# One attention group's transposes through DRAM, eight weight sums four steps earlier, and four weight sums ahead of a copy

## The chip, the cores and the metric

The kernel runs on one core of one Trainium2 chip. The metric is device time in microseconds (us), the median of three runs. Times on the trace's axis are microseconds from the start of the profiled span.

## The reference

Chunked attention (4 batches, 8 heads, 576 positions, head width 64, chunks of 64) feeds two MLPs in turn, on 2304 tokens of width 512.

```python
scores = scale * np.matmul(q_c, k_c.transpose(0, 1, 2, 4, 3))
attn = np.exp(scores - scores.max(-1))            # then divided by its row sum
x = np.matmul(attn, v_c)                          # as (2304, 512)
h = x @ w_in                                      # 512 x 2048
x = (np.maximum(h, 0) + alpha * np.minimum(h, 0)) @ w_out
out = ((x @ w_a) * (x @ w_b)) @ w_o               # 512 x 1536, 1536 x 512
```

The weights come as 64-bit floats. Every product is made of three matmuls on a high and a low part of its operands.

## The kernel before

**Order.** The kernel writes its order by hand: each engine does its instructions in the order in which the code issues them. All DMAs are issued by SP, in that order too. The 2304 tokens are five blocks (512, 256, 512, 512, 512 tokens; numbers 0 to 4). In the first stage, blocks 0, 1 and 2 pass through the first MLP in 16 steps j each: `s1(j)` is the product with `w_in`'s part j (into a PSUM bank `psh`), `prelu` makes `gh` and `gl` of it (ACT `neg` and `pos`, DVE `pos`, ACT `gh`, DVE `gl`), and `s2(j)`, two steps later, multiplies them by `w_out`'s part j into `acc`. Then blocks 3 and 4 pass as a pair through `group1(jp)`, eight groups that need seven products where eight would be plain. They work on sums and differences of the weights (`t_steps`) and of the inputs (`y_sums`). The second MLP and its own groups follow.

**Attention in block 2.** While block 2 runs, `att_line` does the attention of the last eight groups of 128 tokens (units 10 to 17, `us[0]` to `us[7]`). Its tables give a slot to each piece of work; step j calls the slots 2j and 2j + 1. For a unit, `load_kq` loads k and q into a staging buffer, `apart` (ACT `kqd`, two activations) parts each number into its two 16-bit halves and writes them to DRAM (`rowsk`, `rowsq`), `turn_qk` reads them back as DMA transposes (`kT`, `qT`), `multiply` does the scores on PE (`psSO<-kT,qT`; called S below, S15 for unit 15), `soften` the softmax. The sixth, unit 15 (`us[5]`), is the exception: `att_kq` (line 310) transposes its k and q on PE at slot 13, into two of the four `ps` banks, and ACT copies them out.

**Weight sums.** `w_in`'s parts in one piece, high plus low, are needed again by `group1`. `keep_sum(j)` adds them on DVE (line 161, tile `wi`), `keep_out(n)` writes the next n sums to DRAM (`wd`). Parts 0 to 7 are summed in block 1. In block 2, lines 1336 to 1340 sum part j at the end of step j for j = 8 to 15, and write one sum at step 0 and up to two at each of the steps 11 to 15. `load_raw(jp)` reads two of them back (`wir`).

**First pair group.** `group1(0)` (from line 1428) is where the pair begins: `soon` holds the high and low part of one weight tile for the next group (`Txh`, `Txl`), `more` the four sums (`wit`) and the remaining parts (`txh`, `txl`). `p5` and `t2` share a staging buffer; there are three such buffers, and `end1(2)` has just used two of them for block 2's result (`xs`, written out as `x2d`).

**Buffers.** 72 tiles of 128x512 hold weights, attention and sums alike; a new tile waits until the last reader of its buffer is through.

Of the kernel before, what the change touches and what calls it, by code (L numbers as in the profile page):

```python
# [18 lines left out]
def chunk_attention_prelu_mlp_bilinear_mlp(  # L19
# [27 lines left out]
    J1 = F1 // P  # L47
# [38 lines left out]
    def to_hi(hi, lo, src):  # L86
        nc.scalar.activation(out=hi, in_=src, func=AF.Copy)  # L87
# [69 lines left out]
    def keep_sum(j):  # L157

        hi, lo = W["i", j]
        x = wtile("wi", F32)  # L160
        nc.vector.tensor_tensor(out=x, in0=hi.bitcast(F32), in1=lo.bitcast(F32), op=ALU.add)
        whole.append((j, x))

    def keep_out(n):
        for _ in range(min(n, len(whole))):
            j, x = whole.pop(0)
            nc.sync.dma_start(out=wd[j], in_=x)
# [48 lines left out]
    att = {}  # L216
# [83 lines left out]
    def att_T(u, nms="kq"):  # L300
        for nm in nms:
            src = att.pop((nm, u))
            ps = att_bank(u, "psT")
            for g in range(KD):
                nc.tensor.transpose(ps[:, g * P:(g + 1) * P], src[:, g * P:(g + 1) * P], ident)
            t = wtile(f"{nm}T{u}", F32)
            nc.scalar.activation(out=t, in_=ps, func=AF.Copy)
            att[nm + "T", u] = lambda r, g, c, t=t: t[r, half(2 * g + c)]

    def att_kq(u):  # L310
        att["k", u], att["q", u] = att.pop(("kq", u))
        att_T(u)

    def att_S(u, pss=None):
        qT, kT = att.pop(("qT", u)), att.pop(("kT", u))
# [760 lines left out]
    def att_line(bx, x, ut, sums_of):  # L1076

        t0, n = blocks[bx]
        us = range(t0 // P, NU)
        LAG = 3  # L1080

        def dest(u):
            if u * P < t0 + n:
                return *x, u * P - t0
            ut[u] = wtile(f"x{u}", F32).rearrange("p (k t) -> p k t", k=KD)
            return ut[u], None, 0

        def out_of(u, pss):
            o = att_O(u, *dest(u), pss)
            if u + 2 < NU:  # L1090
                load_v(u + 2)
            return o

        def multiply(w):
            pss = [bank("psSO") for _ in range(2)]
            now, then_ = us[w:w + 1], us[max(w - LAG, 0):max(w - LAG + 1, 0)]
            for u in now:
                att_S(u, [ps[:, :KD * CH] for ps in pss])
            o = sum((out_of(u, [ps[:, KD * CH:] for ps in pss]) for u in then_), [])
            each(to_hi, o)  # L1100

            def after():
                for u in now:
                    att_M(u)
                each(to_lo, o)

            return after

        def soften(u):
            att_X(u)  # L1110
            return lambda: weave(att_N(u))

        def out_only(*ws):
            pss = [bank("psSO") for _ in range(2)]
            o = sum((out_of(us[w], [ps[:, i * KD * CH:(i + 1) * KD * CH] for ps in pss])
                     for i, w in enumerate(ws)), [])
            each(to_hi, o)
            return lambda: each(to_lo, o)

        def only(fn, *a):  # L1120
            def step():
                fn(*a)
                return lambda: None

            return step

        at = {
            "S": (0, 3, 6, 10, 13, 16, 19, 22), "turn": (5, 8, 11, 14), "out": (17, 19, 21, 25),
            "apart": (None, None, 1, 5, 7, None, 13, 17), "load": (None, None, None, 1, 4, 7, 10, 13),
        }  # L1130
        steps = [(slot, lambda w=w: multiply(w)) for w, slot in enumerate(at["S"])]
        steps += [(slot, only(apart, u)) for u, slot in zip(us, at["apart"]) if slot]
        steps += [(slot + 1, lambda u=u: soften(u)) for u, slot in zip(us, at["S"])]
        steps += [(slot, only(att_PT, u, True)) for u, slot in zip(us, at["turn"])]
        steps += [(slot + 2, only(att_PT_in, u)) for u, slot in zip(us[KD:], at["out"])]
        steps += [(slot + 2, only(turn_qk, u)) for u, slot in zip(us, at["apart"]) if slot]
        steps += [(slot, only(att_PT_out, u)) for u, slot in zip(us[KD:], at["out"])]
        steps += [(13, only(att_kq, us[5]))]
        steps += [(slot, only(load_kq, u)) for u, slot in zip(us, at["load"]) if slot]
        steps += [(slot, lambda w=w: out_only(w)) for w, slot in ((5, 24), (6, 26), (7, 29))]  # L1140
        steps += [(slot, only(fn)) for slot, fn in sums_of]
        return sorted(steps, key=lambda s: s[0])

    with tc.manual_schedule():
# [60 lines left out]
        bx, by = pairs[1]  # L1205
# [70 lines left out]
        for b, (t0, n) in enumerate(blocks[:bx]):  # L1276
            nxt = xtiles("x")
            if b + 1 < bx:
                steps = att_steps(b + 1, nxt)
            else:  # L1280
                XP["x"] = nxt
                for nm_, k0 in (("11", 0), ("12", 2)):
                    XP[nm_] = [tuple(t[:, k0 + kk, :] for t in nxt) for kk in range(2)]
                first_t = {}

                def begin_t():
                    sums_, first_t["split"] = t_steps(0)
                    TX[0] = [(wtile("txh"), wtile("txl"))]
                    for _, fn in sums_ + first_t["split"].pop(0):
                        fn()  # L1290

                steps = att_line(bx, nxt, ut, (
                    (20, lambda: load_raw(0)), (29, begin_t),
                    (23, lambda: y_sums(0)), (25, lambda: y_sums(1)), (27, lambda: y_sums(2)), (31, lambda: y_sums(3)),
                ))

            def advance(slot, steps=steps):
                rest = []
                while steps and steps[0][0] <= slot:
                    rest.append(steps.pop(0)[1]())  # L1300
                return rest

            def settle(rest):
                for then in rest:
                    then()

            for j in range(J1):
                if b == 0:
                    if j in (1, 3):
                        load_qk(n0 + j // 2)  # L1310
                    if j in (4, 6):
                        load_v(n0 + j // 2 - 2)
                h = h0[0][:, :n] if not (b or j) else s1(j, x, n)
                if b == 0:
                    g = prelu_unpacking(j, h, lambda: w_dma(min(2 * j + 9, NU1)), lambda: advance(2 * j), settle)
                else:
                    rest = advance(2 * j)
                    g = prelu(j, h)
                    settle(rest)

                def second(b=b, j=j, g=g, n=n):
                    if j == 0:
                        acc[0] = new_acc()
                    s2(j, g, acc[0], n)
                    if j == J1 - 1:
                        end1(b, acc[0], n)

                pend.append(second)
                flush(2)
                settle(advance(2 * j + 1))  # L1330
                if b == 1:
                    if j % 2:
                        keep_sum(j // 2)
                    else:
                        keep_out(1)
                if b == bx - 1 and j >= J1 // 2:
                    keep_sum(j)
                    keep_out(2 * (j > 10))
                elif b == bx - 1 and not j:
                    keep_out(1)  # L1340
            x = nxt

        before_mlp2()
# [11 lines left out]
        def product1(ps, jp, q, w, start):  # L1355
            for kk in range(2):
                f = slice(w % 2 * Q + kk * P, w % 2 * Q + (kk + 1) * P)
                (wh, wl), (xh_, xl_) = (t[:, f] for t in TX[jp % 2][w // 2]), XP[q][kk]
                for i, (a, b_) in enumerate(((wh, xh_), (wh, xl_), (wl, xh_))):
                    nc.tensor.matmul(  # L1360
                        out=ps, lhsT=a, rhs=b_, start=(start and kk == 0 and i == 0),
                        stop=(kk == 1 and i == 2), skip_group_check=not start,
                    )
# [34 lines left out]
        def group1(jp):  # L1398
# [6 lines left out]
            more = []  # L1405
            if jp + 2 < J1 // 2:
                load_raw(jp + 2)
            if jp + 1 < J1 // 2:
                more, four = t_steps(jp + 1)
# [22 lines left out]
            if jp == 0:  # L1432
# [5 lines left out]
                product1(B, jp, "s2", 5, True)  # L1438
                tt(t1, p1, B)
                to_hi(*g0)  # L1440
                product1(D, jp, "s1", 4, True)
                p5, t2 = staged("p5")
                copied(p5, D)
                to_lo(*g0)
                for _, fn in soon:
                    fn()
                later(0, g0)
                product1(B, jp, "s3", 6, False)
                tt(t2, p1, B)
# [212 lines left out]
```

## Time and profile before

| what | before |
|---|---|
| median of 3 runs | 862.92 us (860.26 to 863.46) |
| the profiled execution | 863.39 us, span 861.5 us |
| busy PE, DVE, ACT | 841.5, 658.6, 407.7 us |
| mean granted TensorE clock | 0.996 |
| chain that ended last | PE 79%, DVE 10%, ACT 5%, DMA 3% |

Busy is the time in which an engine has an instruction under way. The chain that ended last is followed back from the last instruction; each piece is what the next one waited for. The granted clock is a share of 2.4 GHz. Block 2 with the last attention runs from about 175 to 290 us, the pair's first group from about 286 to 302 us.

### The profile page before, as it was taken

The numbers are of one execution on the slowest core, as the hardware profiler recorded it, in microseconds if no ns is written. First come the engines' busy times: TensorE is split into PE (matmuls) and PEld (weight loads), VectorE is DVE, ScalarE is ACT, GpSimd is POOL, SyncE is SP. The second block draws the span as 40 slices with busy tenths as digits, with TensorE's granted clock in tenths as the row PEclk, the third lists the DMA queues.
The fourth block names the chain that finished last, engine by engine and source line by source line (L and its number), as shares of the span: only waits on it lengthen the run. The fifth ranks groups of instructions, "written<-read, shape, count | busy, mean of one in ns | idle before, by whom it ended". The sixth has DMA issues, their size and how long they took to land.

```text
span 861.5 us, 14497 instructions
## 1 busy us (share of the span) xinstructions
PE 841.5 (98%) x5454; PEld 719.4 (84%) x5454; DVE 658.6 (76%) x1269; ACT 407.7 (47%) x777; POOL 0.7 (0%) x6
## 2 busy tenths in 40 slices
PE   7899999999999899999999999999999999999998
PEld 6778889987787688888888888888888888889998
DVE  5999975655478796867977898898898858848781
ACT  4687775655456454544744333332233225634440
POOL 0000000000000000000000000000000000000000
PEclk9999999999999999999999999999999999999999
DMA  9696779679373421232840354364364238926421
GB/s 218 167 263 209 198 169 233 165 166 197 87 171 112 147 99 49 74 105 95 299 138 31 127 203 142 135 232 141 135 232 141 87 137 308 297 77 184 136 74 49
DMA packets 160854, 134.14 MB, mean 156 GB/s; under 512 B 92176, under 2 KB 128528, under 8 KB 160784
## 3 DMA queue, kind: packets, MB, share of 16 engines
q1 hardware_dynamic: 160784, 133.21, 52.4%
q8 instruction: 43, 0.70, 0.4%
q14 instruction: 27, 0.22, 0.1%
HBM read 82.32 MB, written 44.04 MB: 147 GB/s over the span
## 4 chain that ended last, share of the span: by engine, by line
PE 79%; DVE 10%; ACT 5%; DMA 3%; issue 2%; SPq 0%; DVEq 0%; ACTq 0%
PE acc L403 22%; PE psA L621 8%; PE psD L621 8%; PE psB L621 8%; PE psh L403 6%; PE psr L403 4%; PE psE L621 4%; PE psD L765 3%; PE psB L765 3%; PE psA L765 3%; PE psB L1360 3%; PE psD L1360 2%; PE psA L1360 2%; PE psE L765 2%; DVE wx L148 1%
## 5 line engine op out<-in xcount | busy, mean ns | idle before, releaser
L423 DVE SCALAR_TENSOR_TENSOR pos<-neg,nalpha_sb,pos 128x512 f32<-128x512 f32 (+1 forms) x48 | 31.6, 658 | 34.3 <-ACT pos L422 34.3
L148 DVE SCALAR_TENSOR_TENSOR wx<-wx,wz 128x512 int32<-128x512 int32 x68 | 46.8, 688 | 13.5 <-ACT wx L136 11.6
L87 ACT ACTIVATE gh<-pos 128x512 fp32r<-128x512 f32 (+1 forms) x56 | 32.0, 572 | 41.6 <-DVE pos L423 35.1
L92 DVE TENSOR_TENSOR gl<-pos,gh 128x512 fp32r<-128x512 f32 (+1 forms) x56 | 34.5, 616 | 21.8 <-ACT gh L87 21.1
L651 DVE TENSOR_TENSOR t<-p,psB 128x512 f32<-128x512 f32 x48 | 32.9, 685 | 21.1 <-PE psB L621 16.9
L655 ACT ACTIVATE p<-psA 128x512 f32<-128x512 f32 x24 | 14.4, 599 | 71.7 <-PE psA L621 71.7
L136 ACT ACTIVATE wx<-raw 128x512 f32<-128x512 f32 x68 | 42.5, 671 | 0.6 <-DMA raw<-in_moe_w_out_dram 0.6
L661 ACT ACTIVATE p<-psD 128x512 f32<-128x512 f32 x24 | 14.4, 599 | 50.9 <-PE psD L621 42.4
L140 DVE TENSOR_SCALAR wz<-raw 128x512 uint16<-128x512 uint16 x68 | 31.3, 460 | 0.1
L145 DVE TENSOR_SCALAR wz<-raw 128x512 uint16<-128x512 uint16 x68 | 30.9, 454 | 0.0
L689 ACT ACTIVATE b_sb<-psr 128x256 f32<-128x256 f32 x12 | 4.6, 385 | 53.0 <-PE psr L403 52.1
L421 ACT ACTIVATE neg<-psh 128x512 f32<-128x512 f32 (+1 forms) x48 | 24.8, 518 | 5.3 <-PE psh L403 5.2
L403 PE MATMUL psr<-xrh,Tl 128*128 128x256 f32 x96 | 27.2, 283 | 0.0
L403 PE MATMUL psr<-xrl,Th 128*128 128x256 f32 x96 | 27.2, 283 | 0.0
L403 PE MATMUL psr<-xrh,Th 128*128 128x256 f32 x96 | 27.1, 282 | 0.0
L1374 DVE SCALAR_TENSOR_TENSOR pos<-neg,beta_sb,psA 128x512 f32<-128x512 f32 x8 | 6.0, 748 | 26.1 <-ACT neg L1370 26.1
L422 ACT ACTIVATE pos<-psh 128x512 f32<-128x512 f32 (+1 forms) x48 | 25.2, 525 | 0.0
L269 ACT ACTIVATE kqd<-kq 128x1024 uint16<-128x1024 uint16 x22 | 22.0, 1049 | 0.7 <-DMA kq<-in_k_dram 0.7
L1370 ACT ACTIVATE neg<-p 128x512 f32<-128x512 f32 x24 | 15.2, 633 | 8.8 <-DVE p L1403 7.8
L403 PEld LDWEIGHTS psr<-xrh,Th 128*128 128x128 f32 x96 | 18.4, 192 | 0.4
L403 PEld LDWEIGHTS psr<-xrl,Th 128*128 128x128 f32 x96 | 18.4, 192 | 0.4
L1374 DVE SCALAR_TENSOR_TENSOR p<-neg,beta_sb,p 128x512 f32<-128x512 f32 x24 | 18.0, 749 | 0.8
(946 smaller groups left out, 2967.3 us busy)
## 6 DMA issues: line engine op xcount, KB each, us to landing
raw<-in_moe_w_out_dram SPq DMA_DIRECT2D x28, 512.0 KB, 3.6
raw<-in_moe_w_in_dram SPq DMA_DIRECT2D x16, 512.0 KB, 5.1
raw<-in_moe_w_a_dram SPq DMA_DIRECT2D x12, 512.0 KB, 5.0
raw<-in_moe_w_b_dram SPq DMA_DIRECT2D x12, 512.0 KB, 4.8
cd<-t SPq DMA_DIRECT2D x24, 256.0 KB, 2.3
cd<-p SPq DMA_DIRECT2D x24, 256.0 KB, 2.0
v<-in_v_dram SPq DMA_DIRECT2D x16, 256.0 KB, 4.6
wd<-wi SPq DMA_DIRECT2D x16, 256.0 KB, 2.5
```

Source lines behind the costliest of these rows:

```text
L87: nc.scalar.activation(out=hi, in_=src, func=AF.Copy)
L92: nc.vector.tensor_tensor(out=lo, in0=src, in1=hi.bitcast(F32), op=ALU.subtract)
L136: return nc.scalar.activation(out=x.bitcast(F32), in_=hw.bitcast(F32), func=AF.Copy, scale=2.0 ** -112)
L140: yield nc.vector.tensor_scalar(out=z2[:, :, 0], in0=h2[:, :, 1], scalar1=13, scalar2=None, op0=ALU.logical_shift_right)
L145: yield nc.vector.tensor_scalar(out=z2[:, :, 1], in0=h2[:, :, 3], scalar1=1 << 15, scalar2=None, op0=ALU.bitwise_and)
L148: yield nc.vector.scalar_tensor_tensor(out=x, in0=x, scalar=3, in1=z, op0=ALU.logical_shift_left, op1=ALU.bitwise_or)
L403: nc.tensor.matmul(out=ps, lhsT=a, rhs=b, start=(i == 0 and first), stop=(i == n_i - 1 and a is wl))
L423: yield nc.vector.scalar_tensor_tensor(out=pos, in0=neg, scalar=nalpha_sb[:, j:j + 1], in1=pos, op0=ALU.mult, op1=ALU.add)
L621: nc.tensor.matmul(out=ps, lhsT=a, rhs=b, start=(start and kk == 0 and i == 0), stop=(kk == 1 and i == 2), skip_group_check=not start,)
L651: nc.vector.tensor_tensor(out=out, in0=a, in1=b, op=op)
L765: nc.tensor.matmul(out=ps[:, s * HALF:(s + 1) * HALF], lhsT=a, rhs=x[:, e], start=(start and s == 0 and i == 0 and n == 0), stop=(i == J2 ...
L1360: nc.tensor.matmul(out=ps, lhsT=a, rhs=b_, start=(start and kk == 0 and i == 0), stop=(kk == 1 and i == 2), skip_group_check=not start,)
```

## The change

It has three parts. Unit 15's k and q go the way of the others: `apart` at slot 11 and `turn_qk` at slot 13, and `att_kq` is gone. The sums of `w_in`'s parts 8 to 15 are made in steps 4 to 11 in place of 8 to 15, and written at the steps 9 to 13 in place of 11 to 15. In `group1(0)`, the high part of `soon` goes ahead of the copy of `p5`, then `gl` of the first half, the four sums `wit` and the low part of `soon`, and one more high part (`txh`) behind the copy.

```diff
-    def att_kq(u):
-        att["k", u], att["q", u] = att.pop(("kq", u))
-        att_T(u)
...
-            "apart": (None, None, 1, 5, 7, None, 13, 17), "load": (None, None, None, 1, 4, 7, 10, 13),
+            "apart": (None, None, 1, 5, 7, 11, 13, 17), "load": (None, None, None, 1, 4, 7, 10, 13),
...
-        steps += [(13, only(att_kq, us[5]))]
...
-                if b == bx - 1 and j >= J1 // 2:
-                    keep_sum(j)
-                    keep_out(2 * (j > 10))
-                elif b == bx - 1 and not j:
-                    keep_out(1)
+                if b == bx - 1:
+                    if 0 <= j - J1 // 4 < J1 // 2:
+                        keep_sum(j + J1 // 4)
+                    keep_out({0: 1, 9: 1, 10: 1, 11: 2, 12: 2, 13: 2}.get(j, 0))
...
                 to_hi(*g0)
+                soon[0][1]()
+                to_lo(*g0)
+                for _ in range(4):
+                    more.pop(0)[1]()
+                soon[1][1]()
                 product1(D, jp, "s1", 4, True)
                 p5, t2 = staged("p5")
                 copied(p5, D)
-                to_lo(*g0)
-                for _, fn in soon:
-                    fn()
+                more.pop(0)[1]()
                 later(0, g0)
```

ACT in steps 5 to 7 of block 2, before (the digits behind a name are unit or part, then the tile's number):

```order
L87 ACTIVATE gh_2965<-pos_2960 128x512
L343 ACTIVATE e13_2969<-e13_2969 128x512
L363 ACTIVATE eT12_2996<-psP_2991 128x512
L421 ACTIVATE neg_3018<-psh_3004 128x512
...
L269 ACTIVATE kqd_3077<-kq16_2957 128x1024 x2
L307 ACTIVATE kT15_3089<-psT_3084 128x512
L307 ACTIVATE qT15_3096<-psT_3091 128x512
L343 ACTIVATE e14_3101<-e14_3101 128x512
```

and with the change:

```order
L87 ACTIVATE gh_2967<-pos_2962 128x512
L269 ACTIVATE kqd_2992<-kq15_2852 128x1024 x2
L339 ACTIVATE e13_2971<-e13_2971 128x512
L359 ACTIVATE eT12_3005<-psP_3000 128x512
L417 ACTIVATE neg_3029<-psh_3015 128x512
...
L269 ACTIVATE kqd_3088<-kq16_2959 128x1024 x2
L339 ACTIVATE e14_3102<-e14_3102 128x512
```

The two copies of unit 15's transposes are gone from behind unit 16's `kqd`, and two activations of unit 15 stand ahead of unit 13's exponential.

SP's queue at the same place, before:

```order
L252 DMA kq16_2957<-in_q_dram 128x8x64
L232 DMA v13_3072<-in_v_dram 64x8x64 x2
L271 DMA rowsk16_3079<-kqd_3077 128x1024
L271 DMA rowsq16_3082<-kqd_3077 128x1024
L252 DMA kq17_3098<-in_k_dram 128x8x64
L252 DMA kq17_3098<-in_q_dram 128x8x64
L276 DMA_TRANSPOSE kT16_3158<-rowsk16_3079 128x4x256
L276 DMA_TRANSPOSE qT16_3160<-rowsq16_3082 128x4x256
```

and with the change:

```order
L252 DMA kq16_2959<-in_q_dram 128x8x64
L271 DMA rowsk15_2994<-kqd_2992 128x1024
L271 DMA rowsq15_2997<-kqd_2992 128x1024
L232 DMA v13_3083<-in_v_dram 64x8x64 x2
L271 DMA rowsk16_3090<-kqd_3088 128x1024
L271 DMA rowsq16_3093<-kqd_3088 128x1024
L276 DMA_TRANSPOSE kT15_3095<-rowsk15_2994 128x4x256
L276 DMA_TRANSPOSE qT15_3097<-rowsq15_2997 128x4x256
L252 DMA kq17_3099<-in_k_dram 128x8x64
L252 DMA kq17_3099<-in_q_dram 128x8x64
L276 DMA_TRANSPOSE kT16_3161<-rowsk16_3090 128x4x256
L276 DMA_TRANSPOSE qT16_3163<-rowsq16_3093 128x4x256
```

Unit 15's transposes stand behind unit 16's rows, which wait for unit 16's `kqd`, and ahead of unit 17's loads and unit 16's transposes.

DVE in the pair's first group, before:

```order
L92 TENSOR_TENSOR gl_3965<-pos_3963,gh_3964 128x512
L92 TENSOR_TENSOR Txl_3866<-wir_3873,Txh_3865 128x512
L1403 TENSOR_TENSOR p5_3981<-p1_3947,psB_3934 128x512
L1403 TENSOR_TENSOR p1_3947<-p1_3947,psD_3935 128x512
L1226 TENSOR_TENSOR wit_4002<-wir_3874,wir_3873 128x256
L1226 TENSOR_TENSOR wit_4002<-wir_3874,wit_4002 128x256
L1226 TENSOR_TENSOR wit_4005<-wir_3874 128x256
L1226 TENSOR_TENSOR wit_4005<-wir_3873,wit_4002 128x256
L92 TENSOR_TENSOR txl_3912<-wit_4002,txh_3911 128x512
```

and with the change:

```order
L92 TENSOR_TENSOR gl_3962<-pos_3960,gh_3961 128x512
L1221 TENSOR_TENSOR wit_3974<-wir_3871,wir_3870 128x256
L1221 TENSOR_TENSOR wit_3974<-wir_3871,wit_3974 128x256
L1221 TENSOR_TENSOR wit_3977<-wir_3871 128x256
L1221 TENSOR_TENSOR wit_3977<-wir_3870,wit_3974 128x256
L92 TENSOR_TENSOR Txl_3863<-wir_3870,Txh_3862 128x512
L1397 TENSOR_TENSOR p5_3987<-p1_3944,psB_3931 128x512
L1397 TENSOR_TENSOR p1_3944<-p1_3944,psD_3932 128x512
L92 TENSOR_TENSOR txl_3909<-wit_3974,txh_3908 128x512
```

The four sums stand ahead of the three instructions that they stood behind, two of which wait for products of this group.

## Rows read from the trace of the kernel before

**Rows 1.** Who PE waited for, 174 to 306 us: total, times, longest.
```profile
PE psh L403 <- ACT kT L307: 2.1, 1, 2.1
PE acc L403 <- ACT gh L87: 1.2, 1, 1.2
...
PE psB L1360 <- ACT txh L87: 0.9, 1, 0.9
PE psE L1360 <- DVE Txl L92: 0.7, 1, 0.7
PE psD L1360 <- ACT p L1419: 0.7, 1, 0.7
```
**Rows 2.** Busy time by stretch: PE, PEld, DVE, ACT, POOL (instructions), granted clock, DMA share, GB/s.
```profile
222.30:225.90 3.60, 3.60 (x10) 2.77 (x9) 0.00 (x0) 0.14 (x1) 0.00 (x0) 0.53 1.13 232
...
302.50:454.00 151.50, 151.50 (x669) 125.00 (x668) 117.65 (x206) 76.07 (x135) 0.00 (x0) 1.00 0.36 122
```
**Rows 3.** The chain that ended last, 176 to 306 us: start, length, what.
```profile
217.90 0.48 PE psSO L379 x32
...
221.49 4.61 PE psh L403 x12
...
232.02 0.62 PE psSO L322 x32
...
233.12 2.95 PE acc L403 x12
```
**Rows 4.** ACT's timeline: start, length, instruction, idle time before it and what ended it.
```profile
213.60 0.63 ACT L343 ACTIVATE e<-e 128x512 f32<-128x512 f32 x1 [2.08 <-DVE e L337]
...
269.81 0.61 ACT L422 ACTIVATE pos<-psh 128x512 f32<-128x512 f32 x1
...
276.12 0.58 ACT L422 ACTIVATE pos<-psh 128x512 f32<-128x512 f32 x1
```
**Rows 5.** SP's timeline: its DMA issues.
```profile
220.97 0.36 SPq L271 DMA_DIRECT2D rowsq<-kqd  x1
...
222.68 1.78 SPq L276 DMA_TRANSPOSE kT<-rowsk  x1
224.55 1.25 SPq L276 DMA_TRANSPOSE qT<-rowsq  x1
...
289.19 0.87 SPq L1213 DMA_DIRECT2D wir<-wd  x2
290.95 0.92 SPq L501 DMA_DIRECT2D x2d<-xs  x2
```
**Rows 6.** Tile qT, 176 to 256 us: time from a transposing DMA's issue to landing.
```profile
DMA to landing us min/median/max: 3.3/3.4/3.8
```
**Rows 7.** DMA issues, 176 to 306 us: KB each, median us to landing.
```profile
x2d<-xs SPq DMA_DIRECT2D x2, 512.0 KB, 5.4
```
**Rows 8.** DVE's timeline; pos and wi of steps 7, 11, 13, 14 and 15, the pair's first wit.
```profile
228.18 0.75 DVE L423 SCALAR_TENSOR_TENSOR pos<-neg,nalpha_sb,pos 128x512 f32<-128x512 f32 x1 [7.28 <-ACT pos L422]
...
253.78 0.75 DVE L423 SCALAR_TENSOR_TENSOR pos<-neg,nalpha_sb,pos 128x512 f32<-128x512 f32 x1 [2.57 <-ACT pos L422]
...
270.45 0.75 DVE L423 SCALAR_TENSOR_TENSOR pos<-neg,nalpha_sb,pos 128x512 f32<-128x512 f32 x1
...
277.20 0.74 DVE L423 SCALAR_TENSOR_TENSOR pos<-neg,nalpha_sb,pos 128x512 f32<-128x512 f32 x1
...
281.32 0.69 DVE L161 TENSOR_TENSOR wi<-wi14h,wi14l 128x512 f32<-128x512 f32 x1
281.92 0.75 DVE L423 SCALAR_TENSOR_TENSOR pos<-neg,nalpha_sb,pos 128x512 f32<-128x512 f32 x1
...
288.06 0.68 DVE L161 TENSOR_TENSOR wi<-wi15h,wi15l 128x512 f32<-128x512 f32 x1
288.67 1.28 DVE L92 TENSOR_TENSOR Txl<-wit,Txh 128x512 fp32r<-128x512 f32 x2
...
299.05 0.42 DVE L1226 TENSOR_TENSOR wit<-wir 128x256 f32<-128x256 f32 x1
```

## The prediction, made before the changed kernel ran

> **What bounds the kernel now.** I read the waits of PE first, since PE has an instruction under way for nearly the whole span: where it stands still, or runs slowly, is where time can be had. From 302.5 to 454 us it is busy for all of the 151.5 us at the full granted clock [rows 2]. So behind the pair's first group the kernel goes as fast as PE, and what is won before 302 us should reach the end undiminished. Ahead of it, in the stretch that the change touches, PE waits five times for more than half a microsecond [rows 1]: 2.1 us before a `psh` of step 7, for ACT's copy of `kT`; 1.2 us for `gh`, 0.7 for `Txl`, 0.7 for the copy of `p5`, 0.9 for `txh`. Each of the three parts of the change lies beside one or two of these.
>
> The second view is the chain of waits. There the `psh` of step 7 takes 4.61 us where a product of twelve matmuls behind 64x64 ones takes 2.95 [rows 3]. The third, busy time by stretch, says why: from 222.3 to 225.9 us the granted clock is 0.53, about the lower of its two levels (1.2 GHz), and this follows upon the 2.1 us stop [rows 1, 2]. Last I read the timelines of ACT, SP and DVE for what the moved work meets.
>
> **Part one, unit 15.** Removed from PE: eight transposes, the wait behind them, and the slow product. The last attention matmuls of slot 13 end at 217.90 + 0.48 = 218.38; the slow `psh` ends at 221.49 + 4.61 = 226.10. Without the transposes it starts at 218.38 and takes 2.95, to 221.33: 4.77 us less. Its bank needs no new wait: the transposes took the two banks that ACT had left earlier, and `psh` now gets one of these.
>
> Added on ACT: two activations `kqd` ahead of unit 13's exponential. That one started at 213.60 after 2.08 us of idle time, waiting for DVE [rows 4], and each earlier pair took about 2 us. They fit; cost 0, or up to 2 us later `gh` if k and q came late (they are loaded four slots earlier). Two copies leave ACT behind unit 16's `kqd`.
>
> Added on SP: two writes and two transposes. The writes go out before unit 16's. The transposes wait in the queue behind unit 16's rows, which need unit 16's `kqd`, so they can't be issued before 220.97 + 0.36 = 221.33 [rows 5]. Unit 16's pair started 1.87 us apart (222.68 and 224.55), so `qT15` starts by about 223.2 and lands 3.3 to 3.8 later [rows 5, 6]: 226.5 to 227.0. S15 stood at 232.02 [rows 3] and comes at 232.02 - 4.77 = 227.25. That is a margin of 0.3 to 0.8 us. I take a wait of 0.3, for the margin is thin; the ends are 0 and 1. Queued behind the new transposes are unit 17's loads and unit 16's transposes, each some 3 us later; unit 16's scores are nearly 10 us behind S15, so they should not wait. **Part one: 4.77 - 0.3 = 4.5 us won; 3.8 to 4.8.**
>
> On the one side, the row has PE standing and slowed around its own transposes; on the other, the trace has the DMA's transposes hidden if issued early enough. The Trainium skill (VectorE: DVE Perf Modes, Rules for kernel authors) speaks against the change: it would have TensorE transpose 128x128 where PSUM can take it, and the DMA only otherwise. Its section on the three transpose paths gives 1309 ns for a 128x128 block of 16-bit numbers by DMA; by that, sixteen blocks one after another would be an estimated 20.9 us, and S15 would stand some 15 us, which would make the sum about 870 us. No row bears that out: every transposing DMA of a tile landed within 3.8 us of its issue [rows 6].
>
> **Part two, the sums.** Four sums come to steps 4 to 7, where DVE has room (it stood 7.28 us ahead of step 7's `pos` [rows 8]): cost 0, and 0.6 each if that cover were gone. Steps 8 to 11 keep one each. Steps 12 to 15 lose four, at 0.60 from start to start (281.32 to 281.92 [rows 8]). This is the stretch in which DVE runs almost without a gap, but not every sum counts there. Behind part 12's sum `pos` began at 270.45, and ACT's half of it had ended only at 269.81 + 0.61 = 270.42: nothing won. Behind part 13's, `pos` began at 277.20 and ACT had ended at 276.12 + 0.58 = 276.70: 0.47 won, with the usual 0.03 between. Part 14's brings its full 0.60 [rows 4, 8]. So `gh` of step 15 comes 1.07 earlier, and of PE's 1.2 us 1.07 goes. Then part 15's sum stands right ahead of `Txl` (288.06 to 288.67): 0.6 of PE's 0.7 goes. **Part two: 1.07 + 0.60 = 1.67 us; 0.6 to 2.1**, the low end if only the last sum counts.
>
> The other side of it are the buffers: up to eight sums now lie in the 72 tiles for some steps more. Where a tile is short, DVE waits in its order and the step behind it is late. I price this at 0, as block 2 frees two weight tiles with each step, and keep 1 us for the range.
>
> **Part three, the first pair group.** `p5` is copied late. In the code it stands ahead of the product at whose end it began, so that is not what it waited for; it needs the staging buffer from which the first `x2d` is written. That was issued at 290.95 [rows 5] and such a write takes 5.4 us [rows 7]. Two loads of `wir` went out just ahead of it, at 289.19, because the queue had stood on the last sum. With the sums written earlier these loads are long done, and 0.5 MB less is ahead of `x2d`'s 0.5: I take the 0.7 us wait as gone (this is really part two's doing). The four sums `wit` began at 299.05 [rows 8], behind two instructions that wait for products; now they follow `gl`, some four microseconds earlier, so `txh` is there when PE comes: 0.9 us won. Both could stay if the loads were late. **Part three: 0.7 + 0.9 = 1.6 us; 0 to 1.7.** What would be late next is `gh` of the second half, about 1 us behind.
>
> **Sum.** 4.5 + 1.7 + 1.6 = 7.8 us off the profiled execution's 863.39: 855.6. That execution lay 0.5 above the median of the runs shown, 862.92, so against the median the forecast is 862.92 - 7.8 = **855.1 us**.
>
> **The rivals.**
>
> *The transposes are late.* Unit 15's transposes share the DMA engines with unit 16's rows just when they are fullest (share 1.13 from 222.3 [rows 2]), and S15's margin is under a microsecond. If S15 stands as long as PE did before, 2.1 us, and the next product again runs at the lower clock (4.61 - 2.95 = 1.66 more), 3.8 of part one's 4.8 go: 855.1 + 3.5 = 858.6. Against it, the landing times vary little. Chance 0.15.
>
> *The gain is given back.* DVE is the bound of steps 11 to 15, and PE, 4.8 us earlier, only waits longer for `gh`. Then parts two and three alone are left: 862.92 - 3.3 = 859.6. For it speaks how dense DVE is there; against it that DVE stood 2.57 us ahead of step 11's `pos`, for ACT and so for PE [rows 8]: the dense stretch begins when PE delivers, and moves with it. Chance 0.11.
>
> *SP falls behind, and it is slower.* The new pair pushes unit 17's loads and the transposes of units 16 and 17 back, and S15, S16 and S17 all wait, each with the 2.1 us stop and the slow 1.66: 3 x 3.8 = 11.4 against 8.1 won without any wait, so 862.92 + 3.3 = 866.2. It is slower from the point at which the new stops, slow products included, sum up to more than 8.1 us. Against it are the distances between the scores. The page's 20.9 us, where I named it, would have come out on this side as well. Chance 0.04.
>
> **How the numbers follow.** The forecast has 0.70, with 853.6 to 857.6 as its own range: every wait in the sum gone, and another 1.5 us for how far runs of this kernel lie apart; or part three's 1.6 and some of a late S15 missing. A measurement can tell about 0.5% of this kernel, 4.3 us, from no change, so faster means under 858.6. Faster: 0.70, half of the first rival and a fifth of the second, 0.80. Slower means over 867.2, for which the third rival's stops must sum up to 12.4 us: half of its chance, 0.02. The rest is 0.18. The range reaches over the first two rivals: 853.4 to 860.4.
>
> **What would show it.** Right: no `psT` behind block 0's and 1's; the `psh` of step 7 takes 2.95 us in the chain, at a granted clock of 1.00; S15 begins at about 227.3 and waits less than 0.5 us; DVE's first y sums begin some 4.8 us earlier; PE waits under 0.3 us for `gh` of step 15 and for `Txl`, and not for `p5` and `txh`. Wrong: a wait of S15 for a DMA with a granted clock near one half behind it; sums that wait for a buffer in steps 4 to 8; a wait of ACT in front of unit 17's `kqd`; a new wait of PE in steps 12 to 15 that is longer than the one removed.

## The result and the profile after

| what | after |
|---|---|
| median of 4 runs | 855.28 us (853.6 to 856.06), beside it before 862.78 |
| ratio to before | 0.9916, 95% interval 0.989 to 0.9941 |
| the profiled execution | 856.06 us, span 854.3 us |
| busy PE, DVE, ACT | 839.3, 658.4, 408.6 us |
| mean granted TensorE clock | 0.996 |

The change saves 7.5 us by the medians (5.1 to 9.5 by the ends of the interval); the forecast was 855.1, and the time lies in its range.

The waits of PE from 174 to 300 us, in the profile after, all of them (who waits, for whom: total, times, longest):

```profile
PE acc L399 <- ACT gh L87: 0.2, 1, 0.2
PE acc L399 <- DVE gl L92: 0.2, 1, 0.2
PE psSO L318 <- DMA qT<-rowsq: 0.2, 1, 0.2
```

The five waits of [rows 1] are gone but for 0.2 us of the one for `gh`. The wait for `qT` is not unit 15's: it stands before S12, at 194.9 us, ahead of all that the change moves. The kernel before has a wait there too, 1.0 us at 195.0, a sixth one over half a microsecond that the prediction left out; in the profiles of this case it reads 0.2 to 1.0 us, whatever the kernel. The chain from 214 to 228 us and, from the busy times by stretch, the stretch in which the clock had been low (columns as in [rows 2]):

```profile
217.81 0.47 PE psSO L375 x32
218.28 2.95 PE psh L399 x12
221.23 0.44 PE psP L357 x4
...
227.16 0.62 PE psSO L318 x32
```
```profile
222.30:226.00 3.70, 3.70 (x18) 3.05 (x17) 1.99 (x3) 1.61 (x4) 0.00 (x0) 1.00 0.86 170
```

The `psh` of step 7 follows at once upon the attention and takes 2.95 us where [rows 3] has 4.61; the granted clock is 1.00 where [rows 2] has 0.53; S15 comes at 227.16 for 232.02.

The work that took the transposes' place, on ACT and then in SP's queue:

```profile
211.33 1.99 ACT L269 ACTIVATE kqd<-kq 128x1024 uint16<-128x1024 uint16 x2
213.51 0.63 ACT L339 ACTIVATE e<-e 128x512 f32<-128x512 f32 x1 [0.19 <-DVE e L333]
```
```profile
220.88 0.34 SPq L271 DMA_DIRECT2D rowsq<-kqd  x1
221.32 1.33 SPq L276 DMA_TRANSPOSE kT<-rowsk  x1
222.76 1.24 SPq L276 DMA_TRANSPOSE qT<-rowsq  x1
...
225.36 2.38 SPq L276 DMA_TRANSPOSE kT<-rowsk  x1
```

Unit 15's `kqd` fills the hole ahead of unit 13's exponential: 0.19 us of idle time are left of 2.08 [rows 4]. Its `qT` is issued at 222.76 and, by the trace's landing time for this one transpose (3.6 us), is there at 226.4, 0.7 us ahead of S15's first matmul at 227.09.

To add up gains over several runs I use landmarks in PE's timeline: the start of the first matmul of a piece, before minus run, less the same difference at step 6's `psh`. That last subtraction is needed because the profiled executions are already up to 1.07 us ahead of or 0.38 behind the kernel before at step 6, where nothing of the change has reached PE yet. Gains so far, in us, at each landmark (the runs are told one by one below):

| run | step 8 | `s2(15)` | third `psE` | D's second product | group 1's `acc` | last matmul |
|---|---|---|---|---|---|---|
| the change | 4.77 | 5.86 | 6.46 | 6.90 | 8.34 | 7.31 |
| the change again | 4.78 | 5.83 | 6.44 | 6.75 | 8.20 | 8.04 |
| part one alone | 4.78 | 4.78 | 4.78 | 5.10 | 5.10 | 3.91 |
| part two alone | 0.0 | 1.05 | 1.65 | 2.19 | 2.32 | 1.89 |
| part three alone | 0.0 | 0.0 | 0.0 | 0.0 | 1.43 | 1.31 |
| parts two and three | 0.11 | 1.17 | 1.77 | 2.31 | 3.89 | 2.99 |
| copies first | 3.39 | 3.41 | 3.41 | 4.15 | 4.16 | 3.60 |
| turned late | 4.77 | -1.09 | -0.48 | 0.06 | 1.64 | 1.19 |
| loads first | 4.78 | 4.57 | 5.18 | 5.69 | 7.20 | 6.84 |
| `g` four ahead | 4.77 | 5.85 | 6.46 | 6.85 | 8.31 | 8.49 |
| `g` four ahead again | 4.77 | 5.83 | 6.43 | 6.96 | 8.50 | 8.51 |
| `g` four, `c` five ahead | 4.77 | 5.85 | 6.45 | 6.96 | 8.54 | 8.33 |

### The profile page after: what moved, and what is told of

Its sections match the earlier page's. It is cut to its first block, busy times and chain, and to the rows that moved or that the text cites. A ratio compares the mean times of both kernels' runs of the same rounds, so it can differ in the third digit from the quotient of the medians.

```text
span 854.3 us, 14482 instructions
## 1 busy us (share of the span) xinstructions
PE 839.3 (98%) x5446; PEld 717.8 (84%) x5446; DVE 658.4 (77%) x1269; ACT 408.6 (48%) x777; POOL 0.7 (0%) x6
## 4 chain that ended last, share of the span: by engine, by line
PE 79%; DVE 10%; DMA 5%; ACT 4%; issue 2%; SPq 1%; DVEq 0%; ACTq 0%
PE acc L399 21%; PE psA L617 8%; PE psD L617 8%; PE psB L617 8%; PE psh L399 7%; PE psr L399 4%; PE psE L617 4%; PE psD L761 3%; PE psB L761 3%; PE psA L761 3%; PE psA L1354 2%; PE psD L1354 2%; PE psB L1354 2%; PE psE L761 2%; DVE wx L148 1%
## 5 line engine op out<-in xcount | busy, mean ns | idle before, releaser
L269 ACT ACTIVATE kqd<-kq 128x1024 uint16<-128x1024 uint16 x24 | 24.0, 1048 | 1.2 <-DMA kq<-in_k_dram 1.2
```

## The experiments

**Each part alone.** The first three runs take one part of the diff each into the kernel before, the fourth parts two and three together. Part one alone is this edit:

```diff
-    def att_kq(u):
...
-            "apart": (None, None, 1, 5, 7, None, 13, 17), ...
+            "apart": (None, None, 1, 5, 7, 11, 13, 17), ...
...
-        steps += [(13, only(att_kq, us[5]))]
```

> Part one alone (unit 15's k and q through DRAM; the sums and the first group as before). Theory (part one is worth what its own place shows, and PE carries it to the end): the psh of step 7 takes 2.95 us and step 8 begins 4.8 us earlier; the waits of PE for gh of step 15 (1.2), Txl (0.7), p5 (0.7) and txh (0.9) stay as in the kernel before; 862.8 - 4.7 = 858.1 us, within 0.7. Rival (the gain is given back, for DVE bounds steps 11 to 15): the same 4.8 us at step 8, but the wait for gh of step 15 grows by several microseconds, and the time is 861 to 863 us.

Measured: 859.41 us, ratio 0.9959 (0.9945 to 0.9974). PE's waits of 0.4 us and more, 174 to 306 us (that for `qT` is again S12's):

```profile
PE acc L399 <- ACT gh L87: 1.2, 1, 1.2
PE psB L1355 <- ACT txh L87: 0.9, 1, 0.9
PE psE L1355 <- DVE Txl L92: 0.7, 1, 0.7
PE psSO L318 <- DMA qT<-rowsq: 0.4, 1, 0.4
PE psD L1355 <- ACT p L1414: 0.4, 1, 0.4
```

The 4.78 us arrive whole at `s2(15)`, and the wait for `gh` there is the 1.2 of [rows 1], not several microseconds: the rival that DVE gives it back falls. The time still missed the forecast of 858.1 by 1.3 us. In the table 1.2 us go between group 1's `acc` and the end: 0.36 at about 420 us and 0.85 between 726 and 756 us, by the times of the kernel before. More on these two places below.

Part two alone is the loop over `keep_sum` and `keep_out`:

```diff
-                if b == bx - 1 and j >= J1 // 2:
-                    keep_sum(j)
-                    keep_out(2 * (j > 10))
-                elif b == bx - 1 and not j:
-                    keep_out(1)
+                if b == bx - 1:
+                    if 0 <= j - J1 // 4 < J1 // 2:
+                        keep_sum(j + J1 // 4)
+                    keep_out({0: 1, 9: 1, 10: 1, 11: 2, 12: 2, 13: 2}.get(j, 0))
```

> Part two alone (w_in's last eight sums in steps 4 to 11, written out at steps 9 to 13; unit 15 on PE and the first group's order as before). Theory (the last three sums stand between ACT and PE, and the earlier sums free the queue for x2d): gh of step 15 comes 1.07 us earlier, the 0.7 us wait for Txl nearly goes, and so does the 0.7 us wait for p5, which is not part three's doing; txh's 0.9 us stays; 862.8 - 2.4 = 860.4 us. Rival (p5's wait belongs to the order of the first group): p5's wait stays and the time is 861.1. Second rival (the sums are covered either way): within 0.5 of 862.8, the waits for gh and Txl as before.

Measured: 860.42 us, ratio 0.9974 (0.9963 to 0.9985). It wins 1.05 us at `gh` and 0.60 at `Txl`; of `p5`'s wait nothing is left, `txh`'s 0.9 stays. The theory holds in each place.

Part three alone is the block of the diff in `group1(0)`:

```diff
                 to_hi(*g0)
+                soon[0][1]()
+                to_lo(*g0)
+                for _ in range(4):
+                    more.pop(0)[1]()
+                soon[1][1]()
                 product1(D, jp, "s1", 4, True)
...
-                to_lo(*g0)
-                for _, fn in soon:
-                    fn()
+                more.pop(0)[1]()
```

> Part three alone (the weight sums of the first pair group ahead of the copy of p5; unit 15 on PE and the sums in steps 8 to 15 as before). Theory (part three removes only the wait for txh): txh's 0.9 us goes, p5's 0.7 us stays, for x2d is issued as late as before; the waits for gh of step 15 and Txl stay; 862.8 - 0.9 = 861.9 us. Rival (the new order removes p5's wait as well): 861.2, and no wait of PE for p. Second rival (the weight sums, now ahead, delay the sums behind the first products): p or t1 late, 862.8 or more.

Measured: 861.39 us, ratio 0.9983 (0.9971 to 0.9994). `p5`'s 0.7 us stays, so the rival falls, but the gain in place is 1.43 us and not 0.9. The last product of the first group in PE's timeline shows why, in the kernel before and then in this run:

```profile
299.37 0.39 PE L1360 MATMUL psA<-xh,Txl 128*128 128x512 f32 x1
300.64 0.50 PE L1360 MATMUL psB<-ys2h,txh 128*128 128x512 f32 x1 [0.89 <-ACT txh L87]
300.98 0.40 PE L1360 MATMUL psB<-ys2l,txh 128*128 128x512 f32 x1
301.37 0.50 PE L1360 MATMUL psB<-ys2h,txl 128*128 128x512 f32 x1
```
```profile
299.65 0.39 PE L1360 MATMUL psA<-xh,Txl 128*128 128x512 f32 x1
299.87 0.39 PE L1360 MATMUL psB<-ys2h,txh 128*128 128x512 f32 x1
300.10 0.39 PE L1360 MATMUL psB<-ys2l,txh 128*128 128x512 f32 x1
300.33 0.39 PE L1360 MATMUL psB<-ys2h,txl 128*128 128x512 f32 x1
```

In this run matmuls start every 0.23 us. Before, `psB` started 1.27 us behind its forerunner, 1.04 more than that, though the wait reads 0.89, for a listed wait counts only from the modelled end of the matmul ahead of it. The next start is 0.34 behind, 0.11 more; and the third, 0.39 behind, waits a second time, for `txl`, 0.16 more. With another 0.11 behind that it makes 1.42.

Parts two and three together, with unit 15 left on PE, are both edits above.

> Parts two and three together, unit 15 on PE as before. Theory (the parts add up): no wait of PE for Txl, p5 or txh over 0.3 us, the wait for kT of 2.1 us and the slow psh of 4.61 us as before; 862.8 - 3.3 = 859.5 us. Rival (part one's 4.8 us make room for the others, so that without it they win less): 861 us or more, with a wait for gh of step 15 of over 0.5 us.

Measured: 858.73 us, ratio 0.9954 (0.9937 to 0.9971). That is 0.8 us below the forecast. No wait for `Txl`, `p5` or `txh`, 0.3 for `gh`, and 2.1 for `kT` as before. With part one alone it makes 3.58 + 4.26 = 7.8 us by the medians; the whole change measured 7.5. Within the intervals the parts add up.

**What part one is made of.** Unit 15 stays on PE; only ACT's order changes, its copies now ahead of unit 16's `kqd`:

```diff
+        steps += [(13, only(att_kq, us[5]))]
         steps += [(slot, only(apart, u)) for u, slot in zip(us, at["apart"]) if slot]
...
-        steps += [(13, only(att_kq, us[5]))]
```

> The kernel before with one thing moved: unit 15's transposes stay on PE, but ACT copies them out ahead of unit 16's kqd and not behind it. Theory (of part one's 4.8 us only about 1.1 is the transposes themselves, and 3.7 the stop behind ACT's two kqd and the slow product that follows upon it): the copy of kT begins at about 219.1 and not 220.84, PE stops for under 0.5 us, the granted clock stays at 1.00, the psh of step 7 takes about 3.0 and step 8 begins 3.5 us earlier; 862.8 - 3.4 = 859.4 us. Rival (the lower clock comes with the transposes and the small products, not with the stop): the stop shrinks by 1.8 and the product stays at 4.6, step 8 begins 1.8 us earlier, 861.0 us. Second rival (PE's transposes are what costs): step 8 begins under 0.5 us earlier, 862.5.

Measured: 859.94 us, ratio 0.9964 (0.9952 to 0.9977). Two pieces of its chain, and the stretch that had the low clock:

```profile
218.27 0.54 ACT kT L307
218.81 0.04 issue
218.85 3.06 PE psh L403 x12
```
```profile
222.30:226.00 3.70, 3.70 (x18) 3.03 (x17) 1.30 (x2) 2.21 (x4) 0.00 (x0) 1.00 1.11 226
```

PE stops for 0.25 us instead of 2.10, the clock stays at 1.00, and step 8 begins 3.39 us earlier. So of part one's 4.78, 3.4 are ACT's queue and the slow product behind the stop, and 1.4 are the transposes with their bank. Both rivals fall: the eight transposes are still on PE, and without the long stop the clock stays up and most of the loss is gone. Whether a stop of 2.1 us would lower the clock without transposes just ahead of it, no run shows.

**Late transposes.** In the changed kernel unit 15's `turn_qk` is put behind unit 16's, and in a second kernel only behind unit 17's loads. The table of turns in the first:

```diff
-        steps += [(slot + 2, only(turn_qk, u)) for u, slot in zip(us, at["apart"]) if slot]
+        turns = [(slot + 2, u) for u, slot in zip(us, at["apart"]) if slot]
+        turns = [(s, u) for s, u in turns if u != us[5]]
+        turns.insert([u for s, u in turns].index(us[6]) + 1, (15, us[5]))
+        steps += [(s, only(turn_qk, u)) for s, u in turns]
```

> The changed kernel with unit 15's two DMA transposes behind unit 16's and unit 17's loads in SP's queue: the first rival of the prediction, made to happen. Theory (a late qT15 costs its wait and a product at the lower clock): qT15 is issued at about 228.5 and lands at about 232, S15 stands some 5 us in place of none, the granted clock falls to about one half behind it and a product of twelve takes 1.6 more; 855.3 + 6.5 = 861.8 us. Rival (the stop costs itself alone, the clock stays): 860.2. Second rival (the rest gives it back, for DVE sets the pace of steps 11 to 15): 855.3 to 857.

Measured: 861.28 us (10 runs), ratio 0.9981 (0.9971 to 0.9991); the change's gain is nearly gone. S15 in PE's timeline, and the stretch behind it:

```profile
230.36 1.13 PE L318 MATMUL psSO<-kT,qT 64*64 64x64 f32 x32 [4.18 <-DMA qT<-rowsq]
```
```profile
230.20:236.00 5.80, 5.64 (x73) 4.79 (x74) 1.27 (x2) 2.82 (x6) 0.00 (x0) 0.50 0.10 23
```

The wait is 4.18 us, and the clock is 0.50 for nearly six microseconds behind it. In the table the loss between step 8 and `s2(15)` is 6.95 us against the change (5.86 + 1.09), 2.8 more than the wait; nothing later gives it back but 0.25. The queue had let `qT15` out earlier than I thought (226.54 and not 228.5, though 0.98 of this is the profile's own lead at step 6), so the wait is shorter than the 5 us that I expected; the slow stretch behind it cost 2.8 us and not 1.6.

The second kernel differs in one line:

```diff
-        turns.insert([u for s, u in turns].index(us[6]) + 1, (15, us[5]))
+        turns.insert(0, (14, us[5]))
```

> The changed kernel with unit 17's two loads ahead of unit 15's transposes in SP's queue: the margin by itself. In the profile of the change qT15 is issued at 222.76, lands 3.6 us later at 226.4, and S15 begins at 227.1. Theory (the margin is 0.7 us and nothing else waits): qT15 is issued some 1.3 us later, at 224.0, and lands at 227.6 or some tenths later, behind the loads; S15 waits 0.5 to 1.0 us, the granted clock stays at 1.00 behind it, and the shift at step 8 falls by as much. Rival (a late transpose brings the lower clock at any length of the wait): the product behind S15 takes over 4 us in place of 2.95.

Measured, one run: 856.72 us. `qT15` goes out at 224.71 for 222.76. This profile is 0.20 us behind the one after at step 6, so that is 1.75 us later; S15 waits:

```profile
228.56 0.69 PE L318 MATMUL psSO<-kT,qT 64*64 64x64 f32 x32 [1.21 <-DMA qT<-rowsq]
```
```profile
227.00:232.00 5.00, 3.79 (x76) 3.02 (x75) 1.60 (x3) 1.64 (x4) 0.00 (x0) 1.00 0.91 176
```

S15 comes 1.27 us late against the profile after (228.56 for 227.09, less the 0.20), for a transpose that goes out 1.75 later and takes 3.7 us to land for 3.6: the margin was about 0.6 us. The clock stays at 1.00, and the rival, that a late transpose slows PE at any length of the wait, falls. By the table it costs 1.1 to 1.3 us, behind step 8 and not at it, for S15 stands behind step 8's product.

**What is lost behind 302 us.** In the profile after, the gain falls by 0.65 us at about 413 us, where the second half of a part of `g` is late, and by 0.4 between 709 and 760. The first of the two places:

```profile
412.64 0.50 PE L399 MATMUL acc<-gyh,wo4h 128*128 128x512 f32 x1
413.37 0.50 PE L399 MATMUL acc<-gyl,wo4h 128*128 128x512 f32 x1 [0.22 <-DVE gyl L92]
```

Two runs loaded ahead to cover this: `g` four parts ahead, and with it `c` five ahead.

```diff
-                for j in range(3):
+                for j in range(4):
                     load_g(j)
...
-            load_g(j + 3)
+            load_g(j + 4)
```

> The changed kernel with the second stage's loads of g made four parts ahead in place of three: the part g3 is loaded ahead of the last x2d, and each later one a step of 2.7 us earlier. In the profile of the change the shift falls there from 8.42 to 7.80 us, at g4's low part. Theory (g4 lands late behind x2d and the weights in the queue): the shift stays at 8.4 up to 702 us, PE's 0.2 us wait for gyl is gone, and the time is 0.6 below the changed kernel's: 854.7 us. Rival (what is lost there is not the load but DVE's or ACT's order): the shift falls as before, 855.3.

Measured: 854.74 us, ratio 0.9901 (0.9886 to 0.9917). The gain no longer falls at 413 us (8.31 at group 1's `acc`, 8.49 at the last matmul), and the time is at the forecast of the theory.

The second has `AHEAD = 5` for `AHEAD = 4` besides.

> As the run with g four parts ahead, and with the loads of c in the plain part of the second stage five ahead in place of four. In the profile of the change 0.4 us are lost between 709 and 760 us, in slips of about 0.1 us at c's low parts. Theory (these wait for loads): another 0.4 us less, 854.3 us. Rival (they wait for ACT and DVE, which split c between other work): no difference to the run with g four ahead, 854.7; or slower, if the tile for a fifth c comes free late.

Measured: 854.9 us, ratio 0.9909 (0.9895 to 0.9923). In the stretch from 717 us in the kernel before it takes 0.4 us longer than there; the fifth `c` does not cure the slips.

As the first of these seemed to beat the change by 0.5 us, both ran once more, on one chip:

> The changed kernel itself once more, beside the run with g four ahead on the same chip. Theory (the difference between the two is the wait at g4's low part alone): 855.3 us, with the shift against the kernel before falling by 0.1 to 0.7 us at g4's low part. Rival (the 0.6 us there was one execution's accident): no fall there, and the same time as with g four ahead.

> The changed kernel with g loaded four parts ahead, once more, beside the changed kernel on the same chip. Theory: no wait at g4's low part again, and a time 0.3 to 0.6 us below the changed kernel's, so about 854.8 us, which these rounds can hardly tell from it. Rival: the loads made earlier cost elsewhere, and the time is the changed kernel's or above.

Measured: the change 854.78 us, ratio 0.9918 (0.9906 to 0.9931); `g` four ahead 855.1 us, ratio 0.9922 (0.991 to 0.9934). The unchanged change now shows no fall at 413 us (8.20 at `acc`, 8.21 behind it), and these are all waits of PE in it from 174 to 460 us (that for `qT` is S12's):

```profile
PE psSO L318 <- DMA qT<-rowsq: 0.7, 1, 0.7
PE acc L399 <- ACT gh L87: 0.3, 1, 0.3
PE acc L399 <- DVE gl L92: 0.2, 1, 0.2
```

So the rival of the repeat holds this far: the unchanged kernel need not have the late `gyl`. But it is not an accident of one execution alone: the same wait of 0.2 us is listed in the profiles of part one alone and of the late transposes, and in none of the three with `g` four ahead. There the gain grows by 0.15 to 0.2 us at this place; in the nine profiles with three ahead it changes by -0.6 to +0.15. What loading ahead wins there is too little for the times to show it, and no version here is shown to beat the change.

## Why the prediction was right, point by point

**Part one, 4.5 forecast, 4.8 measured.** The working held to the hundredth (4.77 in the profile after, 4.78 alone). The 0.3 taken off for S15 was not needed: its margin, given as 0.3 to 0.8, is 0.6 to 0.7. ACT's two `kqd` cost nothing, as forecast. One reading behind it was wrong and did no harm: the 3.8 us within which "every transposing DMA of a tile landed" is the longest for `qT` [rows 6]; in the same stretch of the kernel before, `kT` took 3.7 to 4.7 us.

The rule from the Trainium skill that I weighed against it (VectorE: DVE Perf Modes, Rules for kernel authors: a 128x128 transpose on TensorE where PSUM can take it) comes out mixed. The estimate made from its section on the three transpose paths, sixteen blocks one after another and S15 standing some 15 us, is not borne out: S15 did not wait, and the late kernel paid 4.18. What a single block takes, no run here shows. But the run with the copies first shows that transposing on PE was not what cost the kernel before most. With ACT's queue in the right order PE's transposes cost 1.4 us; the DMA wins those only because its landing is hidden.

**Part two, 1.67 forecast, 1.65 measured, of which 0.3 go again just behind.** It splits as said: about 1.06 at `gh`, 0.60 at `Txl`. No sum waited for a buffer, as priced. That part 12's sum would win nothing shows in DVE's timeline after, where its place is taken by a wait for ACT:

```profile
265.57 0.75 DVE L419 SCALAR_TENSOR_TENSOR pos<-neg,nalpha_sb,pos 128x512 f32<-128x512 f32 x1 [0.60 <-ACT pos L418]
```

What I missed is what is late next behind `Txl`. ACT's copy of `p1` from bank A and the product that goes on in that bank, in the profile after:

```profile
283.45 0.58 ACT L1413 ACTIVATE p<-psA 128x512 f32<-128x512 f32 x1
```
```profile
283.64 0.40 PE L1354 MATMUL psE<-y22h,Txl 128*128 128x512 f32 x1
284.08 0.50 PE L1354 MATMUL psA<-xh,txh 128*128 128x512 f32 x1
```

The copy ends at 284.03, and the product begins 0.44 behind the matmul ahead of it and not 0.23; with the 0.11 behind it, 0.3 of the 0.6 go again (the shift against before, here and below without the step 6 difference of 0.09, is 6.55 us at the third `psE` and 6.24 at `psB`).

**Part three, 1.6 forecast, about 2.2 measured.** `p5`: forecast 0.7, measured 0.75 between the start of D's first product (shift 6.24) and of its second (6.99). The copy still waits for the buffer, but PE no longer does:

```profile
289.11 0.60 ACT L1413 ACTIVATE p<-psD 128x512 f32<-128x512 f32 x1 [0.76 <-DMA x2d<-xs]
```

That it is `x2d` is shown. Why `x2d` lands earlier is less sure than the prediction made it. In the nine profiles with part two its first half is issued 2.5 us ahead of D's first product, in the four without part two 2.2 us: 0.3 us are the queue, as the prediction had it. The rest is the time to landing, 4.60 us after for 5.04 before. It lies at 3.8 to 4.7 with part two and at 4.3 to 5.1 without; the 4.3 is the run with the copies first, where the two loads of `wir` still go out just ahead and PE's wait was gone as well. That the `wir` loads set the landing is not settled. `txh`: forecast 0.9, measured 1.44. This is the term that was mis-sized most: a wait was priced by its listed idle time, where PE pays for the restart and for the late `txl` too.

**The sum.** At group 1's `acc` the change has won 8.34 us (8.20 the second time), where the steps summed up to 8.1 without S15's 0.3. The step that failed is that "what is won before 302 us should reach the end undiminished": by the last matmul it is 7.31 in one execution and 8.04 in the other, 3.91 of 5.10 with part one alone, but 8.49 of 8.31 with `g` four ahead. PE gains or loses some tenths at single late parts of `g` and `c`, differently from one profiled execution to the next; a gain ahead of it is known to about a microsecond at the end. The places are two, the late `gyl` and 726 to 756 us by the times of the kernel before; elsewhere no profile's gain moves by 0.1 us, but for one by 0.2 at about 310 us. Why part one alone lost more there, and in all its runs stayed above the forecast, isn't settled. So the mechanism held, but that the median came within 0.2 us of the forecast is in part luck: 0.4 to 0.5 us more was won by 302 us than forecast, and 0.2 to 1.0 us was lost behind it.

**The rivals.** The late transposes were a real danger, priced at 3.8 us for a stop of 2.1; made to happen, a stop of 4.2 costs 6.9 in place and 6.0 in the medians, and one of 1.2 about as much as itself. DVE gave nothing back. SP's queue did not fall behind: unit 16's `kT` is issued 2.7 us later than before (225.36 for 222.68) though PE is 4.8 us ahead, and it took 6.2 us to land for 4.3, its `qT` 4.6 for 3.5. So the landing times did not "vary little"; but that `qT` is there at 232.4, 4.1 us ahead of S16, which shows no wait.

## What to carry to other kernels

When PE stops behind its own small piece of work, look at what stands ahead of the releaser in the releasing engine's queue: here most of the gain of rerouting the work was to be had by swapping two steps of ACT. Price a wait by the distance of starts, not by the listed idle time, and look one instruction further for the operand or the bank that is late next. Before you credit or blame a few tenths far behind the change, profile the same kernel twice.

## What the runs showed of the hardware

The granted clock fell to about one half, the lower of its two levels (1.2 GHz), behind PE's stops of 2.10 us (0.53 over 3.6 us; eight transposes stand just ahead of this stop) and 4.18 us (0.50 over 5.8 us), and stayed at 1.00 behind stops of 1.21 and 0.25 us; the eight transposes with the short stop did not lower it. Unit 15's `qT` landed 3.4 to 3.7 us behind its issue in all eight profiles that transpose it by DMA, whether it went out ahead of unit 17's loads or behind them. Not every such DMA did: unit 16's `kT`, next behind these loads in the profile after, took 6.2 us. And a single listed wait understated what PE lost: the one of 0.89 us cost 1.15 with its slower restart.
